# One quarter of the first block's first GEMM by seven products instead of eight

## The chip, the cores and the metric

The kernel runs on one core of a Trainium2 chip. The time is the device time of one execution, in microseconds (us). It is taken as the median of several runs. One more execution is recorded by the hardware profiler, and all rows and times of day ("at 38.21") below come from that one. The engines are TensorE (PE, with its weight loads as PEld), VectorE (DVE), ScalarE (ACT), GpSimd (POOL) and SyncE (SP, whose queue issues all DMAs here). Each engine works through its own list of instructions in order. An instruction that needs another engine's result waits for a semaphore.

## The reference

Two stages follow each other. First a retention (a linear attention with decay) over 4 batches, 8 heads, 768 positions and 64 dimensions:

```
state = gamma * state + k_t^T v_t
y_t   = scale * q_t state
```

Then y is laid out as x, with 3072 tokens of 512 values, and goes through two GEMMs with an ELU between them:

```
h = x @ w_in                      # 512 -> 2048
g = where(h > 0, h, exp(min(h, 0)) - 1)
out = g @ w_out                   # 2048 -> 512
```

All inputs are fp32, but for the weights, which the host hands over as raw float64 bits, two 32-bit words each.

## The kernel before

**Blocks and quarters.** The tokens are worked on in six blocks of 512. Each block has its retention, its first GEMM and its second GEMM. The hidden width of 2048 is cut for the first GEMM into four quarters, n = 0 to 3. A quarter pairs 256 hidden rows of the upper half (weights `w_a[n]`, row 0) with 256 of the lower half (`w_b[n]`, row 1), and each has the two halves of the 512 inputs. So a quarter is a two by two block product: hidden rows by inputs, with the block's tokens cut in two halves of 256 as the other factor.

**Seven products.** From the second block on, a quarter is computed by Strassen's scheme in Winograd's form: seven products M1 to M7 of 128x128 weights with 256 tokens, four matmuls each, where the plain way takes eight. It needs four sums of weights (s1 to s4, function `combine_w_in`, with s1 written over a21 in `w_b`, and s2, s3, s4 in `w_s`), four sums of x (t1 to t4, `combine_x_parts`), and sums of the products. Products accumulate in PSUM: M6 is added onto M1, M5 onto that, M3 onto that, all in one bank; M4 is added onto M7 in another. Between these steps ACT copies the bank's value out (`kept`), since other sums need it.

**The first block.** Here the kernel starts with nothing in place: weights arrive as 1 MB pieces of raw bits, and x comes out of the retention piece by piece. So the first GEMM of the first block is plain (`plain_first`). Its sixteen tiles, four a quarter, have 128 hidden values and 512 tokens each. Tiles 0 to 4 are begun with the first 256 tokens, as soon as the retention has made these, and finished with the others; tiles 5 to 15 are done at once. Their PSUM banks come from a pool with the tags a (two banks), b and d; tile 4 has one of four banks of the pool `ps_r`, which the retention's scores (sc), states (kv) and outputs (y) use in turn.

**ELU.** Each tile goes through `elu`: ACT takes relu(-h) and its exponential (lines 477 and 478, tile r), and DVE combines them with h (line 481). That last part is put one tile later in DVE's list than ACT's part, and only after it is the bank free.

**Weights.** Piece p (0 to 7 are `w_a[0]`, `w_b[0]`, `w_a[1]`, `w_b[1]` and so on; 8 to 15 belong to the second GEMM and are put into the first two parts of `w_s`) is loaded into one of three staging tiles. ACT prepares it with two operations (lines 164 and 166) and a third multiplication (line 168), which DVE does in its place where `by_vector` is set (line 190). DVE then decodes it (lines 191 and 194), and with that the staging tile is free for the load of the piece three further on.

**The order of the work** is written out by hand: the loop over the generator `inner` (`plain_first`) names for each tile n what else is put into the engines' lists after it: loads of the second block's q, k and v (`load`), the pieces (`next_piece`, which decodes one and prepares the next), the scaling of v on POOL (`scale_v`, line 281), the sums for the second GEMM (`inputs_of_first`), and the second block's scores, states and outputs at tiles 10 to 15. Then follows the first block's second GEMM (`second_of_first`, line 611), and after it the second block's first GEMM, whose quarters take their weight sums from `sides`. Before all this, PE does one matmul of 512 columns and 28 small ones on a tile of zeros, whose results nobody reads (lines 1106 and 1110).

Of the kernel before, what the change touches and what calls it, by code (L numbers as in the profile page):

```python
# [9 lines left out]
FP32 = mybir.dt.float32  # L10
# [4 lines left out]
ALU = mybir.AluOpType  # L15
# [3 lines left out]
def kernel(  # L19
# [32 lines left out]
    nc = tc.nc  # L52
    PSUM = bass.MemoryType.PSUM
    P = nc.NUM_PARTITIONS
# [5 lines left out]
    TH = TB // 2  # L60
# [14 lines left out]
    mpool = ctx.enter_context(tc.tile_pool(name="mpool", bufs=4))  # L75
# [3 lines left out]
    ps_r = ctx.enter_context(tc.tile_pool(name="ps_r", bufs=4, space=PSUM))  # L79
# [6 lines left out]
    so_ = t4.tile([P, 2, 7, 256], FP32, name="so")  # L86
# [35 lines left out]
    w_a, w_b, w_s = ([x[:, n] for n in range(NQ)] for x in (w_a_, w_b_, w_s_))  # L122
# [96 lines left out]
    begin = so_.rearrange("p n s c -> p (n s c)")  # L219
# [3 lines left out]
    for h in range(H):  # L223
# [11 lines left out]
        out=causal, in_=causal, compare_op=ALU.is_gt, fill=1.0, base=0, pattern=[[-1, P]], channel_multiplier=1  # L235
    )
    cmask = const.tile([P, D], FP32, name="cmask")
    for sub in range(2):
        r = slice(sub * D, (sub + 1) * D)
# [25 lines left out]
    xb = const.tile([P, 4, TB], FP32, name="xb")  # L265
    xt_ = const.tile([P, 4, 2, TH], FP32, name="xt")
    xt = [xt_[:, n] for n in range(4)]
# [3 lines left out]
    xt1 = [xb[:, n].rearrange("p (a t) -> p a t", a=2) for n in (1, 2, 3, 0)]  # L271
# [178 lines left out]

    half = [slice(0, TH), slice(TH, TB)]

    def combine_x_parts(tb=None):
        sub = lambda o, x, y: nc.vector.tensor_tensor(out=o, in0=x, in1=y, op=ALU.subtract)
        b11, b12, b21, b22 = (x_of(tb)[:, 2 * r : 2 * r + 2, half[t]] for r in range(2) for t in range(2))
        t1, t2, t3, t4_ = xt1 if tb == 1 else xt
        sub(t1, b12, b11)
        yield
        sub(t2, b22, t1)
        yield  # L460
        sub(t3, b22, b12)
        yield
        sub(t4_, b21, t2)
# [8 lines left out]
    def elu(g, h, depth=1, then=None):  # L472


        r = epool.tile([P, 512], FP32, name="r", tag="r", bufs=3)
        e = r if len(h.shape) == 2 else r.rearrange("p (a c) -> p a c", c=P)
        nc.scalar.activation(e, h, AF.Relu, scale=-1.0)  # L477
        nc.scalar.activation(e, e, AF.Exp, scale=-1.0)  # L478

        def last():  # L480
            nc.vector.scalar_tensor_tensor(g, e, -1.0, h, ALU.add, ALU.max)  # L481
            if then:
                then()

        while len(later) >= depth:
            later.pop(0)()
        later.append(last)

    def plain_first():

        tiles = [(n, w, row, fi) for n in range(NQ) for w, row in ((w_a, 0), (w_b, 1)) for fi in range(2)]
        banks = []

        def part(k, columns):
            n, w, row, fi = tiles[k]
            for j in range(4):
                nc.tensor.matmul(
                    banks[k][:, columns], lhsT=w[n][:, fi, j // 2, j % 2, :], rhs=xb[:, j, columns],
                    start=(j == 0), stop=(j == 3), skip_group_check=True,
                )  # L500

        for k in range(5):
            hp = bank("aabd"[k]) if k < 4 else ps_r.tile([P, 2, TH], FP32, name="hp", tag="r")
            banks.append(hp.rearrange("p a b -> p (a b)"))
            if k == 0:
                part(0, slice(0, C))
                yield
                part(0, slice(C, 2 * C))
            else:
                part(k, half[0])  # L510
            if k:
                yield
        for k in range(5):
            part(k, half[1])
            n, w, row, fi = tiles[k]
            elu(g_plain[row * NF + 2 * n + fi], banks[k])
            yield
        for k, (n, w, row, fi) in enumerate(tiles[5:]):
            hp = bank("aabd"[k % 4]).rearrange("p a b -> p (a b)")
            for j in range(4):  # L520
                nc.tensor.matmul(
                    hp, lhsT=w[n][:, fi, j // 2, j % 2, :], rhs=xb[:, j, :], start=(j == 0), stop=(j == 3)
                )
            elu(g_plain[row * NF + 2 * n + fi], hp)
            yield
        flush()

    def of_first(r, f, t, count=2):

        i = (r * NF + f) % 4  # L530
        g = gq[gnames[(r * NF + f) // 4]]
        return g[:, 2 * i + t] if count == 1 else g[:, 2 * i + t : 2 * i + 4 : 2, :]
# [112 lines left out]
    def combine_w_out(at, low, high):  # L645

        tt = lambda o, x, y, op: nc.vector.tensor_tensor(out=o, in0=x, in1=y, op=op)
        if at < 3:

            ms = [mpool.tile([P, 2, TH], FP32, name="m", tag="m") for _ in range(4)]  # L650
            ms = [m.rearrange("p a (b c) -> p (a b) c", c=P)[:, 0:3] for m in ms]
            ss = gq["T3"].rearrange("p (k f) (b c) -> p k (f b) c", k=4, c=P)
        else:
            ms, ss = (stage.tile([P, 4, 4, P], FP32, name="wi", tag="stage") for _ in range(2))
            ms = [ms[:, k, 0:3] for k in range(4)]
        ss = [ss[:, k] for k in range(4)]
        for first, dst, k in [(0, ms, 0), (3, ss, 1)][:: 1 if at < 3 else -1]:
            a11, a21, a12, a22 = (x[k][:, :, P * d : P * d + P] for x in (low, high) for d in range(2))
            s1, s2, s3, s4 = dst
            tt(s1, a21, a22, ALU.add)  # L660
            yield
            tt(s2, s1, a11, ALU.subtract)
            yield
            tt(s3, a11, a21, ALU.subtract)
            yield
            tt(s4, a12, s2, ALU.subtract)
            to = scratch2[first : first + dst[0].shape[1]].rearrange("j p (k f c) -> k f p j c", k=4, f=4)
            for k in range(4):
                to_send.append((to[k, at], dst[k]))
            yield  # L670

    def combine_w_in(n):

        tt = lambda o, x, y, op: nc.vector.tensor_tensor(out=o, in0=x, in1=y, op=op)
        a11, a12, a21, a22 = w_a[n][:, :, 0], w_a[n][:, :, 1], w_b[n][:, :, 0], w_b[n][:, :, 1]
        s2, s3, s4 = (w_s[n][:, j] for j in range(3))
        tt(s3, a11, a21, ALU.subtract)
        yield
        tt(a21, a21, a22, ALU.add)
        yield  # L680
        tt(s2, a21, a11, ALU.subtract)
        yield
        tt(s4, a12, s2, ALU.subtract)

    def bank(x):
        return ps_f.tile([P, 2, TH], FP32, name="p" + x, tag=x, bufs=2 if x == "a" else 1)

    def kept(ps):
        m = mpool.tile([P, 2, TH], FP32, name="m", tag="m")
        nc.scalar.copy(m, ps)  # L690
        return m
# [85 lines left out]
    for tb in range(1, NTB):  # L777
# [5 lines left out]
        for j in ORDER2:  # L783
            last = (4, 3) if j == 4 and tb == NTB - 1 else (3, 4)
# [321 lines left out]
            nc.tensor.matmul(warm[:, 0:n], lhsT=blank[:, 0:P], rhs=blank[:, 0:n], start=True, stop=True, skip_group_check=True)  # L1106

    unread(1, TB)
    for n in range(28):
        nc.tensor.matmul(  # L1110
            (warm, other)[n % 2][rows(n // 2 % 2), 0:D], lhsT=blank[rows(n % 2), 0:D], rhs=blank[rows(n % 2), 0:D],
            start=True, stop=True, skip_group_check=True,
        )
# [48 lines left out]
    y = outputs(0, 1)  # L1162
# [9 lines left out]
    def run(steps):  # L1172
        for _ in steps:
            pass

    def next_piece(by_vector=False):
        decode_all()
        prepare(by_vector=by_vector)
# [4 lines left out]
    def some(steps, count):  # L1183
        for _ in itertools.islice(steps, count):
            pass

    for n, _ in enumerate(inner):
        if n in (0, 2, 4):
            load(CPB + n // 2)
        if n == 4:  # L1190
            load(CPB + 3)
        if n in (1, 2, 4, 5, 7, 9):
            next_piece(n in (1, 2, 5, 7))
        if n in (3, 5, 7, 9):
            scale_v(CPB + (n - 3) // 2)
        if n == 4:
            run(inputs_of_first(0, [hslot() for _ in range(3)]))
        elif n == 10:
            scores(1, 0)
            scores(1, 1)  # L1200
        elif n == 11:
            states(1, 0)
            states(1, 1)
            next_piece()
            parts = sums_of_pieces(0)
            next(parts)
        elif n == 12:
            outputs_step(1, 0)
            run(parts)
            next_piece()  # L1210
        elif n == 13:
            outputs_step(1, 1)
            smalls = small_of_pieces(0)
            some(smalls, 3)
        elif n == 14:
            outputs_step(1, 2)
            some(smalls, 2)
            decode_all()
        elif n == 15:
            run(smalls)  # L1220
# [43 lines left out]
    def retention_step(tb, step):  # L1264
# [12 lines left out]
    tail = iter(())  # L1277
    last = held["last"]
    sides = [
        itertools.chain(combine_w_in(1), last), itertools.chain(combine_w_in(2), combine_w_in(3)), iter(()), iter(()),  # L1280
    ]
    smalls = {2: combine_small(2), 3: combine_small(3)}
    some(smalls[2], 1)
# [204 lines left out]
```

## Time and profile before

| what | us |
|---|---|
| median of three runs (lowest, highest) | 634.45 (632.83, 636.55) |
| the profiled execution | 632.87 |
| its span, first to last instruction | 630.9 |
| PE busy in the span | 624.8 |
| DVE, ACT, POOL busy | 483.1, 253.3, 21.8 |
| first block's first GEMM from tile 0's second half | 29.58 to 85.20 |
| first block's second GEMM begins | 85.20 |
| second block's first GEMM begins | 133.54 |

The span is what the profile covers; about 2 us lie outside it. A row of a timeline gives the start in us, the duration in us, the engine, the source line, the operation, what it writes and reads with its shape, and how many instructions are merged in the row. A bracket at its end gives the idle time before it and what ended that. An fp32 matmul appears as two records (x8 is four matmuls). A row's duration for PE includes the time for the last result to come out, so what counts is the distance from one start to the next. The tile names are those of the program, such as pa, pb and pd for banks with the tags a, b and d, hp for the bank of tile 4, and gC for the results of the ELU.

### The profile page before, as it was taken

How to read it: one execution, taken by the hardware profiler on the slowest of the kernel's cores; microseconds unless marked ns; L12 is line 12 of the kernel's file. 1: busy time of each engine (PE TensorE's matmuls, PEld its weight loads, DVE VectorE, ACT ScalarE, POOL GpSimd, SP SyncE). 2: the span in 40 equal slices, each digit the busy share in tenths (PEclk: the TensorE clock that was granted, in tenths of full speed). 3: DMA queues.
4: the chain of work that ended last, by engine and by line, in shares of the span. 5: the costliest groups of instructions: out<-in, count | busy, mean ns of one | idle time of the engine just before them, and what ended most of it. 6: DMA issues, size and time to landing. Idle time of an engine off the chain costs nothing.

```text
span 630.9 us, 16128 instructions
## 1 busy us (share of the span) xinstructions
PE 624.8 (99%) x6680; PEld 560.1 (89%) x6680; DVE 483.1 (77%) x884; ACT 253.3 (40%) x472; POOL 21.8 (3%) x25
## 2 busy tenths in 40 slices
PE   8999999999999999999999999999999999999998
PEld 5864578888899999889999989999988999988997
DVE  5779789989789675699685588777489877558975
ACT  6698635015541114653112646111465211366311
POOL 1021000000000000200000200000110000000000
PEclk9999999999999999999999999999999999999999
DMA  8698669689287888405888702888810798600794
GB/s 331 278 406 291 188 210 268 196 267 316 81 311 248 239 255 299 180 2 174 274 266 292 282 2 64 264 284 296 310 73 12 216 308 252 217 18 2 232 309 162
DMA packets 75897, 136.85 MB, mean 217 GB/s; under 512 B 6320, under 2 KB 31792, under 8 KB 70704
## 3 DMA queue, kind: packets, MB, share of 16 engines
q1 hardware_dynamic: 75824, 135.82, 64.8%
q8 instruction: 53, 0.87, 0.5%
q14 instruction: 20, 0.16, 0.1%
HBM read 114.56 MB, written 21.23 MB: 215 GB/s over the span
## 4 chain that ended last, share of the span: by engine, by line
PE 77%; SPq 1%; DVE 1%; DMA 1%; issue 0%; ACT 0%; ACTq 0%; DVEq 0%
PE pa L955 20%; PE pa L913 10%; PE pd L955 10%; PE pb L955 5%; PE pa L867 5%; PE pb L913 4%; PE pa L740 4%; PE qa L913 3%; PE pd L867 2%; PE qd L913 2%; PE pd L913 2%; PE pd L740 2%; PE y L394 1%; PE sc L307 1%; PE y L409 1%; PE kv L338 1%
## 5 line engine op out<-in xcount | busy, mean ns | idle before, releaser
L963 ACT COPY ms<-pa 128x128 f32<-128x128 f32 x104 | 27.7, 266 | 146.7 <-PE pa L955 146.7
L955 PE MATMUL pa<-ts,wq 128*128 128x128 f32 x560 | 74.2, 275 | 0.0
L955 PE MATMUL pd<-ts,wq 128*128 128x128 f32 x552 | 73.5, 276 | 0.0
L955 PEld LDWEIGHTS pa<-ts,wq 128*128 128x128 f32 x560 | 68.5, 192 | 0.4
L955 PEld LDWEIGHTS pd<-ts,wq 128*128 128x128 f32 x552 | 67.1, 192 | 0.6 <-DVE res L967 0.2
L955 PE MATMUL pa<-gC,wq 128*128 128x128 f32 x480 | 64.7, 278 | 0.0
L478 ACT ACTIVATE r<-r 128x512 f32<-128x512 f32 x96 | 60.5, 630 | 3.1
L955 PEld LDWEIGHTS pa<-gC,wq 128*128 128x128 f32 x480 | 59.0, 192 | 1.5 <-issue 0.3
L477 ACT ACTIVATE r<-gC 128x512 f32<-128x512 f32 x64 | 39.9, 624 | 32.4 <-DVE gC L921 32.4
L967 DVE TENSOR_TENSOR res<-pd,ms 128x128 f32<-128x128 f32 x68 | 19.5, 287 | 39.6 <-PE pd L955 38.4
L481 DVE SCALAR_TENSOR_TENSOR gC<-r,gC 128x512 f32<-128x512 f32 x64 | 44.0, 719 | 0.7 <-ACT r L478 0.7
L829 DVE TENSOR_TENSOR ts<-gC,ts 128x512 f32<-128x512 f32 x60 | 41.3, 688 | 1.0
L829 DVE TENSOR_TENSOR ts<-gC 128x512 f32<-128x512 f32 x60 | 41.0, 684 | 0.0
L281 POOL TENSOR_TENSOR chunk<-chunk,vf 128x512 f32<-128x512 f32 x16 | 20.0, 1251 | 428.8 <-DMA chunk<-in_qkv_dram 345.8
L955 PE MATMUL pb<-gC,wq 128*128 128x128 f32 x240 | 31.7, 275 | 0.0
L988 ACT COPY res<-pa 128x128 f32<-128x128 f32 x34 | 9.0, 266 | 55.0 <-PE pa L955 55.0
L955 PEld LDWEIGHTS pb<-gC,wq 128*128 128x128 f32 x240 | 29.2, 192 | 0.0
L690 ACT COPY m<-pa 128x512 f32<-128x512 f32 x24 | 13.9, 581 | 30.2 <-PE pa L740 16.3
L921 DVE TENSOR_TENSOR gC<-qa,gC 128x512 f32<-128x512 f32 x8 | 5.5, 692 | 25.0 <-PE qa L913 18.3
L913 PE MATMUL pa<-xt,w_b 128*128 128x256 f32 x96 | 23.0, 382 | 0.0
L913 PE MATMUL pa<-xt,w_s 128*128 128x256 f32 x96 | 23.0, 382 | 0.0
L913 PE MATMUL pa<-xb,w_a 128*128 128x256 f32 x96 | 22.7, 379 | 0.0
(255 smaller groups left out, 1244.3 us busy)
## 6 DMA issues: line engine op xcount, KB each, us to landing
wq<-scratch_dram SPq DMA_DIRECT2D x277, 256.0 KB, 4.3
chunk<-in_qkv_dram SPq DMA_DIRECT2D x23, 1024.0 KB, 8.6
wraw<-in_w_dram SPq DMA_DIRECT2D x15, 1024.0 KB, 6.0
out_dram<-res SPq DMA_DIRECT2D x14, 256.0 KB, 3.8
scratch_dram<-gT SPq DMA_DIRECT2D x12, 256.0 KB, 4.3
scratch_dram<-m SPq DMA_DIRECT2D x12, 192.0 KB, 6.0
scratch_dram<-so SPq DMA_DIRECT2D x4, 512.0 KB, 4.6
scratch_dram<-wi SPq DMA_DIRECT2D x2, 1024.0 KB, 6.4
```

Source lines behind the costliest of these rows:

```text
L281: eng.tensor_tensor(out=kv[:, 1], in0=kv[:, 1], in1=vf[:, i].unsqueeze(2).to_broadcast([C, H, D]), op=ALU.mult)
L477: nc.scalar.activation(e, h, AF.Relu, scale=-1.0)
L478: nc.scalar.activation(e, e, AF.Exp, scale=-1.0)
L481: nc.vector.scalar_tensor_tensor(g, e, -1.0, h, ALU.add, ALU.max)
L690: nc.scalar.copy(m, ps)
L740: nc.tensor.matmul(ps[:, fi, :], lhsT=w[:, fi, j2, :], rhs=x[:, j2, :], start=(begin and fi == 0 and j2 == 0), stop=(j2 == 1), skip_group_ ...
L829: sub = lambda o, x, y: nc.vector.tensor_tensor(out=o, in0=x, in1=y, op=ALU.subtract)
L867: nc.tensor.matmul(ps[:, f, :], lhsT=lhs[f], rhs=xs[j][k], start=(begin and f == 0), stop=True, skip_group_check=True,)
L913: nc.tensor.matmul(ps[:, fi, :], lhsT=w[:, fi, j2, :], rhs=x[:, j2, :], start=(j in (1, 7) and fi == 0 and j2 == 0), stop=(j2 == 1), skip_ ...
L955: nc.tensor.matmul(ps, lhsT=w[:, f, :], rhs=ts[j][k][:, f, :], start=(begin and f == 0), stop=(f == 3), skip_group_check=True,)
L963: nc.scalar.copy(m, ps)
L967: nc.vector.tensor_tensor(out=o, in0=x, in1=y, op=ALU.add)
```

## The change

The second quarter (tiles 4 to 7) of the first block is now computed by the seven products. A new function `quad_first` holds them. The banks of M1 and M2 come from `ps_r`, the bank of M7 and M4 has the tag a. The first halves (128 hidden values of each row pair) of M1 and M2 stand where tile 4's first half stood, before the second 256 tokens of x are there; the rest follows tiles 0 to 3. The sums of x are made into the tile `so`, which the sums of the second GEMM use later. The sums of weights are made by `combine_w_in(1)` during tiles 2 to 4. Since pieces of the second GEMM are later put over s2 and s3 in `w_s[1]`, these two are made again (`combine_w_in_again`) where `combine_w_in(1)` stood for the second block. Pieces are prepared and decoded at other tiles, and two instead of four of them have their multiplication on DVE. Ten of the 28 small matmuls at the start are gone.

```diff
-        for k in range(5):
-            hp = bank("aabd"[k]) if k < 4 else ps_r.tile([P, 2, TH], FP32, name="hp", tag="r")
-            banks.append(hp.rearrange("p a b -> p (a b)"))
+        for k in range(4):
+            banks.append(bank("aabd"[k]).rearrange("p a b -> p (a b)"))
...
-        for k in range(5):
+        quad = quad_first(1)
+        next(quad)
+        yield
+        for k in range(4):
             part(k, half[1])
             n, w, row, fi = tiles[k]
             elu(g_plain[row * NF + 2 * n + fi], banks[k])
             yield
-        for k, (n, w, row, fi) in enumerate(tiles[5:]):
-            hp = bank("aabd"[k % 4]).rearrange("p a b -> p (a b)")
+        for _ in quad:
+            yield
+        for k, (n, w, row, fi) in enumerate(tiles[8:]):
+            hp = bank("daab"[k % 4]).rearrange("p a b -> p (a b)")
...
+    x_first = [so_.rearrange("p n s c -> p (n s) c")[:, 2 * k : 2 * k + 2] for k in range(4)]
+
+    def quad_first(n):
+
+        a11, a12, s1, a22 = w_a[n][:, :, 0], w_a[n][:, :, 1], w_b[n][:, :, 0], w_b[n][:, :, 1]
+        s2, s3, s4 = (w_s[n][:, j] for j in range(3))
+        b11, b12, b21, b22 = (xb[:, 2 * r : 2 * r + 2, half[t]] for r in range(2) for t in range(2))
+        t1, t2, t3, t4_ = x_first
+        pairs = {1: (a11, b11), 2: (a12, b21), 3: (s4, b22), 4: (a22, t4_), 5: (s1, t1), 6: (s2, t2), 7: (s3, t3)}
+
+        def product(j, ps, begin, tiles=range(2)):
+            w, x = pairs[j]
+            for fi in tiles:
+                for j2 in range(2):
+                    nc.tensor.matmul(
+                        ps[:, fi, :], lhsT=w[:, fi, j2, :], rhs=x[:, j2, :],
+                        start=(begin and fi == 0 and j2 == 0), stop=(j2 == 1), skip_group_check=True,
+                    )
+
+        def use(r, t, h):
+            elu(of_first(r, 2 * n, t), h)
+
+        def with_kept(ps, m):
+            h = mpool.tile([P, 2, TH], FP32, name="m", tag="m")
+            nc.vector.tensor_tensor(out=h, in0=ps, in1=m, op=ALU.add)
+            return h
+
+        pa, pb = (ps_r.tile([P, 2, TH], FP32, name="hp", tag="r") for _ in range(2))
+        product(1, pa, True, [0])
+        product(2, pb, True, [0])
+        yield
+        product(1, pa, False, [1])
+        m1 = kept(pa)
+        product(2, pb, False, [1])
+        use(0, 0, with_kept(pb, m1))
+        product(6, pa, False)
+        u2 = kept(pa)
+        yield
+        pd = bank("a")
+        product(7, pd, True)
+        product(5, pa, False)
+        u4 = kept(pa)
+        use(1, 1, with_kept(pd, u4))
+        yield
+        product(3, pa, False)
+        use(0, 1, pa)
+        yield
+        product(4, pd, False)
+        use(1, 0, with_kept(pd, u2))
+        yield
+
+    def combine_w_in_again(n):
+
+        tt = lambda o, x, y, op: nc.vector.tensor_tensor(out=o, in0=x, in1=y, op=op)
+        s2, s3 = (w_s[n][:, j] for j in range(2))
+        tt(s2, w_b[n][:, :, 0], w_a[n][:, :, 0], ALU.subtract)
+        yield
+        tt(s3, w_b[n][:, :, 1], s2, ALU.subtract)
...
-    for n in range(28):
+    for n in range(18):
...
-        if n in (1, 2, 4, 5, 7, 9):
-            next_piece(n in (1, 2, 5, 7))
+        if n in (0, 4, 5, 6, 7, 9):
+            next_piece(n in (0, 4))
         if n in (3, 5, 7, 9):
             scale_v(CPB + (n - 3) // 2)
-        if n == 4:
+        if n == 0:
+            xparts, wparts = combine_x_parts(0, x_first), combine_w_in(1)
+        elif n == 1:
+            some(xparts, 2)
+        elif n == 2:
+            some(wparts, 2)
+        elif n == 3:
+            some(wparts, 1)
+            some(xparts, 1)
+        elif n == 4:
+            run(wparts)
+            run(xparts)
+        elif n == 6:
             run(inputs_of_first(0, [hslot() for _ in range(3)]))
...
-        itertools.chain(combine_w_in(1), last), itertools.chain(combine_w_in(2), combine_w_in(3)), iter(()), iter(()),
+        itertools.chain(combine_w_in_again(1), last), itertools.chain(combine_w_in(2), combine_w_in(3)), iter(()), iter(()),
```

Two smaller edits go with it: `combine_x_parts` takes the place for its results as an argument, and `elu` reshapes its tile to the form of h, whatever that is.

In the prediction, M1 to M7 are the products; h1, h2 and h3 are the three sums made by `with_kept` (M2 + m1, M7 + u4 and M4 + u2); m1, u2 and u4 are ACT's copies; "ELU k" is the pair of ACT operations of tile k and DVE's end of it.

More of the change, by code (lines that the diff above doesn't have):

```diff
@@ L451, with combine_x_parts @@
     half = [slice(0, TH), slice(TH, TB)]
-    def combine_x_parts(tb=None):
+    def combine_x_parts(tb=None, at=None):
         sub = lambda o, x, y: nc.vector.tensor_tensor(out=o, in0=x, in1=y, op=ALU.subtract)
         b11, b12, b21, b22 = (x_of(tb)[:, 2 * r : 2 * r + 2, half[t]] for r in range(2) for t in range(2))
-        t1, t2, t3, t4_ = xt1 if tb == 1 else xt
+        t1, t2, t3, t4_ = at or (xt1 if tb == 1 else xt)
         sub(t1, b12, b11)
@@ L475, in elu @@
         r = epool.tile([P, 512], FP32, name="r", tag="r", bufs=3)
-        e = r if len(h.shape) == 2 else r.rearrange("p (a c) -> p a c", c=P)
+        e = r if len(h.shape) == 2 else r.rearrange("p (a c) -> p a c", c=h.shape[-1])
         nc.scalar.activation(e, h, AF.Relu, scale=-1.0)
@@ L510, in plain_first @@
                 part(k, half[0])
-            if k:
                 yield
-        for k in range(5):
+        quad = quad_first(1)
+        next(quad)
+        yield
+        for k in range(4):
             part(k, half[1])
```

## The prediction

> **What bounds the kernel now.** First the page: the busy line, then the table of busy time by stretches, to see whether the stage of the change has idle time to win.
>
> ```profile
> span 630.9 us, 16128 instructions
> ...
> PE 624.8 (99%) x6680; PEld 560.1 (89%) x6680; DVE 483.1 (77%) x884; ACT 253.3 (40%) x472; POOL 21.8 (3%) x25
> ```
> ```profile
> 28.00:60.00 32.00, 32.00 (x168) 18.97 (x171) 25.46 (x34) 28.99 (x35) 6.31 (x4) 1.00 0.84 329
> 60.00:86.00 26.00, 26.00 (x466) 14.90 (x457) 20.59 (x38) 14.93 (x20) 0.00 (x0) 1.00 0.59 183
> 86.00:141.00 55.00, 54.91 (x255) 48.02 (x254) 50.97 (x78) 17.81 (x18) 0.00 (x0) 1.00 0.83 243
> ```
> Columns are us, then busy PE, weight load, DVE, ACT, POOL. From 28 us on PE never waits, so its work is the time: a product saved is time saved, a stall is time lost, one for one. But in 28 to 60, where the change lies, ACT is busy 28.99 of 32 us and DVE 25.46, and PE runs unhindered only because four rotating PSUM banks decouple it from them. Next the timelines of that stretch (start, us, engine, line, operation). PE:
>
> ```profile
> 36.49 1.89 PE L497 MATMUL hp<-xb,w_a 128*128 128x256 f32 x8
> 38.21 3.60 PE L521 MATMUL pa<-xb,w_a 128*128 128x512 f32 x8
> ...
> 55.38 3.60 PE L521 MATMUL pa<-xb,w_b 128*128 128x512 f32 x8
> 58.91 2.10 PE L307 MATMUL sc<-chunk 64*64 64x64 f32 x128
> 60.93 3.70 PE L521 MATMUL pb<-xb,w_b 128*128 128x512 f32 x8
> 64.56 2.08 PE L338 MATMUL kv<-chunk 64*64 64x64 f32 x112
> ```
> From start to start, four matmuls of 256 columns take 1.72, a tile of 512 columns 3.43. ACT:
>
> ```profile
> 34.40 1.15 ACT L164 ACTIVATE w_a<-wraw 128x1024 uint32<-128x1024 uint32 x1
> 35.59 1.39 ACT L166 ACTIVATE w_a<-wraw 128x1024 fp8e4<-128x1024 f32 x1
> 36.84 0.56 ACT L477 ACTIVATE r<-pb 128x512 f32<-128x512 f32 x1
> 37.43 0.63 ACT L478 ACTIVATE r<-r 128x512 f32<-128x512 f32 x1
> 37.97 1.14 ACT L164 ACTIVATE w_b<-wraw 128x1024 uint32<-128x1024 uint32 x1
> ...
> 57.56 1.18 ACT L164 ACTIVATE w_s<-wraw 128x1024 uint32<-128x1024 uint32 x1
> 58.78 1.39 ACT L166 ACTIVATE w_s<-wraw 128x1024 fp8e4<-128x1024 f32 x1
> 60.03 1.14 ACT L168 ACTIVATE wraw<-wraw 128x1024 f32<-128x1024 f32 x1
> 61.07 0.58 ACT L477 ACTIVATE r<-pa 128x512 f32<-128x512 f32 x1
> ```
> An ELU pair costs ACT 1.13 (36.84 to 37.97), a piece prepared in two operations 2.44 (34.40 to 36.84), in three 3.51 (57.56 to 61.07). DVE:
>
> ```profile
> 43.71 1.94 DVE L194 CUSTOM_DVE_ANT_0 w_b<-wraw,w_b 128x2048 uint16<-128x2048 uint16 x1
> ...
> 60.34 2.48 DVE L318 TENSOR_TENSOR chunk<-sc,cmask 128x512 f32<-128x512 f32 x4
> 62.74 0.68 DVE L481 SCALAR_TENSOR_TENSOR gC<-r,pa 128x512 f32<-128x512 f32 x1
> 65.76 0.43 DVE L350 TENSOR_TENSOR chunk<-kv,carry 128x256 f32<-128x256 f32 x1 [2.34 <-PE kv L338]
> ```
> The masks (L318) end at 62.8, PE's states (L338), which reuse the scores' PSUM tiles, begin at 64.56: a margin of 1.7 us. The same timeline gives an ELU's end 0.60 from start to start, an add or subtract of 128x512 0.61, or 0.72 when the next needs it, a decode 1.89 (33.40 to 35.29) and 2.60 with the multiplication on DVE (52.25 to 54.85). Handovers: PE's results reach ACT 0.2 after the last matmul's slot ends (29.58 plus 1.73, then ACT at 31.51), ACT's and DVE's reach others after 0.04.
>
> [...] here L829 and L561 take 684 to 690. [...] every start above follows program order, so an instruction that waits holds all behind it. [...] L194 at 43.71 took 1.94 instead of 1.23 while POOL worked from 43.01 to 44.57[...].
>
> **The change, part by part.** Removed from PE: tile 4 in two halves and tiles 5 to 7, 3.45 + 3 x 3.43 = 13.74. Added: seven products of 1.73, 12.09. Half of M1 and M2 takes the place of tile 4's first half, at 27.78, with the same columns. Unhindered, tile 8 would begin at 36.49 + 1.73 (the other halves) + 5 x 1.73 = 46.87 instead of 48.51: a credit of 1.64.
>
> But where tiles had banks of their own, M6, M5 and M3 accumulate in M1's bank, and ACT must have copied it before each. So I lay out the three queues in their new order, each start being the later of engine free and inputs ready. Until 30.2 nothing differs.
>
> M6 needs M1's copy, s2 and t2. ACT: ELU 0 at 31.51, then piece 4's two operations now stand ahead of ELU 1: 32.66 to 35.09, ELUs 1, 2, 3 to 38.54, M1's copy (0.58, as L690) done 39.1. DVE: piece 3 to 32.1, ELU 0 at 32.80, t1 and t2 to 34.8, then a wait for ELU 1's exponential till 36.38, s3 36.98, s1 37.70, ELU 2 38.31, s2 38.91 to 39.60. M6 starts at 39.64 and not 38.21: stall 1.43.
>
> M7 41.36 and M5 43.09 find all ready (t3 done 40.2, u2's copy 42.6). M3 waits for u4's copy: M5 ends 44.82, copied 45.02 to 45.60, M3 at 45.64: stall 0.82 (s4, behind piece 4's decode, is done 44.6). M4 47.36. Tile 8 49.09, tile 9 52.52, due to end at 55.95.
>
> Tile 10 needs the bank of M7 and M4, free only after the add h3 = M4 + u2. DVE: h2 45.64 (behind u4), an ELU, piece 5 to 49.46, an ELU to 50.06; piece 6 waits for ACT. ACT: ELU of h2 46.37, piece 6 47.52 to 51.1 with three operations. So piece 6 decodes 51.14 to 53.02, the four second-GEMM inputs to 55.79, h3 55.79 to 56.48, tile 10 at 56.52: stall 0.57. Scores 59.95, tile 11 61.97, its end 65.60.
>
> States need the masks done. ACT: ELU of M3 51.00, piece 7 52.15 to 55.63 (three operations, two before), ELU of h3 56.52, piece 8 57.67 to 61.15 (three, two before), ELU 8 61.15. DVE waits for that with tile 8's end till 62.44, then piece 8 63.04, ELU 9 64.92, masks 65.52 to 68.0. States begin at 66.84 (first two masks) and need the fourth 0.20 later: stall 1.24 + 0.20. Tile 12 starts at 69.04 where it was 66.57.
>
> Sum: 1.43 + 0.82 + 0.57 + 1.44 - 1.64 = +2.6 us. From here DVE has idle time (2.34 and more before L350, 1.99 before L384 at 81.34), the queues meet again at L384, and the second GEMM starts about 87.8 instead of 85.20. What follows is tied to it and shifts whole.
>
> Priced at nothing: (a) the weight loads on SP. Pieces 7 to 11 are asked for when 4 to 8 are decoded, at 43.96, 49.5, 53.1, 58.9, 65.0 (before 38.70, 45.71, about 51.1, 54.9, 59.8); at the page's 6.0 to landing they meet ACT's need at 52.15, 57.67, 63.45, 69.5, 74.1 with 2.2 us or more; behind a late one would queue an ELU and so tile 12. (b) the later weight combination, four DVE operations down to two: PE is busy 39.00 of 39.00 from 141 to 180, so the 2 x 0.69 show nowhere; without that cover they would give 1.4. (c) ten dummy matmuls: the first scores start at 5.15, when their chunk, issued at 0.74, landed (4.4 later). Dummies pass at about 0.03 a record, twenty records, so PE now idles from some 4.4 to 5.15. Below nothing isn't possible, as the chunk sets the start. [...] I take 0, since the hole is short. (d) POOL's blocking: four L281 of 1.3 to 1.8, seen to cost DVE 0.71 and 0.24; on the new path 0 to about 1.5; I take 0.
>
> **Rivals.** A, not slower: ACT and DVE keep up, no stall, -1.64, 632.8. For it, PE's earlier freedom; against, ACT's 90% in that stretch, with three copies of 0.58 and two L168 of 1.1 added. Each copy would have to be ready before its product, M1's 1.4 us earlier. B, slower: POOL's L281, whose chunks are now fetched ahead of piece 7, block DVE between 37.7 and 46, on the path to s2 and h2. At 0.71 a hit (L194 above) one or two hits add 0.7 to 1.4: +3.3 to +4.0, 637.8 to 638.5; it decides from 0.6 on. Against: in the trace two of four cost little. C, half the loss: DVE reaches the masks 1.4 us sooner, because piece 8 or ELU 8 goes faster than priced; then +1.2, 635.6. Against: three ACT operations at 3.5 are seen four times. That the saving isn't made can't be: four matmuls in 32 are gone.
>
> **How the numbers follow.** The profiled execution was 632.87 (span 630.9 and 2.0 around); it would be 635.5, span 633.5. The median of the runs, 634.45, lies 1.6 above it, so I predict 634.45 + 2.6 = 637.0. My case 0.60 (own range 635.6 to 638.2), B 0.17, C 0.16, A 0.04, a rest of 0.03 faster. About 0.5%, 3.2 us, is what can be told from no change: slower is B and the 0.18 of my case above 637.6, together 0.35; same 0.62; faster 0.03. The range 634.6 to 639.4 takes in C, B and the unpriced 1.4, and leaves out A.
>
> **What would show it.** PE idle of about 1.4 ahead of M6 (released by DVE or ACT), 0.8 ahead of M3 (ACT copy), 0.6 at tile 10 (DVE), 1.2 at the states (DVE L318); tile 8 starting near 49.1; the second GEMM near 87.8 and no new stall after. I am wrong if these sum to under 1.6, if kv after 7 us is slower than 0.69, or if DVE runs dry of slack between 86 and 141, where it is busy 93%.

## The result, and the profile after

| | before | changed |
|---|---|---|
| median, us (lowest, highest) | 633.95 (632.51, 636.55) | 639.18 (637.76, 641.29) |
| ratio, 95% interval | 1 | 1.009 (1.0069 to 1.011) |
| the profiled execution, span | 632.87, 630.9 | 640.92, 639.0 |

The changed kernel is slower by 0.9%, where I had called "no measurable difference" the likeliest case. The page of the changed kernel, the same lines as before:

```profile
span 639.0 us, 16131 instructions
...
PE 625.8 (98%) x6676; PEld 563.8 (88%) x6676; DVE 488.5 (76%) x891; ACT 256.7 (40%) x477; POOL 21.2 (3%) x25
```
PE issued four records fewer and yet was busy 1.0 us longer, and it was idle in the span for 639.0 - 625.8 = 13.2 us instead of 6.1. Where, the table by stretches tells (columns as in the prediction: the stretch, its length, busy PE, weight load, DVE, ACT and POOL, then the clock granted to PE, the DMA share and GB/s):

```profile
28.00:60.00 32.00, 28.88 (x155) 21.40 (x146) 27.05 (x38) 23.96 (x30) 5.50 (x4) 0.95 0.71 278
60.00:86.00 26.00, 25.01 (x463) 14.07 (x463) 22.18 (x39) 22.02 (x27) 0.00 (x0) 1.00 0.64 200
86.00:141.00 55.00, 54.44 (x292) 45.32 (x290) 47.89 (x73) 17.34 (x17) 0.00 (x0) 1.00 0.77 228
...
42.00:44.00 2.00, 1.98 (x6) 1.68 (x7) 2.00 (x4) 0.86 (x2) 0.00 (x0) 0.68 1.01 426
44.00:46.00 2.00, 2.00 (x6) 1.59 (x5) 1.93 (x3) 1.26 (x3) 0.75 (x1) 0.50 1.03 434
46.00:48.00 2.00, 2.00 (x10) 1.74 (x10) 2.00 (x3) 1.97 (x2) 1.44 (x2) 0.97 1.01 422
```
PE lacks 3.1 us between 28 and 60 and 1.0 between 60 and 86. And something appears that neither the busy columns nor the waits of another engine hold: from about 42 to 46 us the clock falls to half. Now PE's own timeline:

```profile
24.94 0.68 PE L394 MATMUL y<-chunk 64*64 64x64 f32 x26
27.02 0.75 PE L394 MATMUL y<-chunk 64*64 64x64 f32 x35 [1.40 <-issue]
...
38.00 1.89 PE L689 MATMUL hp<-xb,w_a 128*128 128x256 f32 x8
42.02 3.09 PE L689 MATMUL hp<-so,w_s 128*128 128x256 f32 x8 [2.13 <-DVE w_s L736]
44.91 2.49 PE L689 MATMUL pa<-so,w_s 128*128 128x256 f32 x8
...
49.80 1.99 PE L689 MATMUL hp<-xb,w_s 128*128 128x256 f32 x8 [0.68 <-ACT m L752]
...
60.72 3.70 PE L524 MATMUL pa<-xb,w_b 128*128 128x512 f32 x8 [0.33 <-DVE m L699]
...
70.52 0.33 PE L338 MATMUL kv<-chunk 64*64 64x64 f32 x4 [0.45 <-DVE chunk L318]
71.03 2.34 PE L338 MATMUL kv<-chunk 64*64 64x64 f32 x108 [0.17 <-DVE chunk L318]
...
91.93 1.24 PE L614 MATMUL x<-gC,w_s 128*128 128x256 f32 x5
...
141.24 1.99 PE L802 MATMUL pa<-xt,w_a 128*128 128x256 f32 x8 [0.81 <-DVE m L598]
148.93 1.35 PE L802 MATMUL pa<-xb,w_b 128*128 128x256 f32 x5 [0.51 <-ACT m L752]
```
In this order: M6 (42.02), M7 (44.91), M3 (49.80), tile 10 (60.72) and the states (70.52, 71.03) have the stalls that were forecast, with the forecast releasers. While M6 waited, PE started nothing else: from 40 to 42 us it has no matmul (busy 0.00, x0). M6 and M7 take 2.89 and 2.33 from start to start instead of 1.73: the half clock (0.68 from 42 to 44, 0.50 from 44 to 46). The row at 27.02 is new in kind. The bracket names no engine and no DMA: "issue" is time in which PE waited for nothing that the profile shows. It lies in the first block's outputs, where the change touched nothing; a smaller one, 0.44 us, stands at 13.41. The kernel before has in the same place:

```profile
24.81 1.50 PE L394 MATMUL y<-chunk 64*64 64x64 f32 x63
```
I cut each trace at two landmarks, the first matmul on the hp bank (the quarter's M1, before: tile 4) and the start of the second GEMM (91.93, before 85.20):

| stretch | before | changed | difference |
|---|---|---|---|
| start to the hp bank | 27.78 | 29.29 | +1.5 |
| hp bank to second GEMM | 57.42 | 62.64 | +5.2 |
| second GEMM to end | 545.70 | 547.07 | +1.4 |

Only the middle was in my sum, with +2.6. It holds the half clock as well, 1.76 us of it (2.89 + 2.33 - 2 x 1.73). The +1.4 at the end are nearly all in the two waits at 141.24 and 148.93 (0.81 + 0.51).

### The profile page after: what moved, and what is told of

It is laid out like the page before. It is cut to its first block, busy times and chain, and to the rows that moved or that the text cites. A ratio compares the mean times of both kernels' runs of the same rounds, so it can differ in the third digit from the quotient of the medians.

```text
span 639.0 us, 16131 instructions
## 1 busy us (share of the span) xinstructions
PE 625.8 (98%) x6676; PEld 563.8 (88%) x6676; DVE 488.5 (76%) x891; ACT 256.7 (40%) x477; POOL 21.2 (3%) x25
## 4 chain that ended last, share of the span: by engine, by line
PE 76%; SPq 1%; DVE 1%; DMA 1%; issue 0%; ACT 0%; ACTq 0%; DVEq 0%
PE pa L1017 20%; PE pa L975 10%; PE pd L1017 10%; PE pb L1017 5%; PE pa L929 5%; PE pb L975 4%; PE pa L802 4%; PE qa L975 3%; PE pd L929 2%; PE qd L975 2%; PE pd L975 2%; PE pd L802 2%; PE y L394 1%; PE sc L307 1%; PE y L409 1%; PE kv L338 1%
```

## The experiments

All ratios are to the kernel before, run on the same chip at the same time. Each profiled execution is cut at the same two landmarks (us):

| kernel | median | ratio (95%) | to hp | hp to 2nd GEMM | to end |
|---|---|---|---|---|---|
| changed, again | 640.90 | 1.0115 (1.010 to 1.013) | 29.30 | 61.14 | 548.1 |
| changed, 28 dummies | 639.35 | 1.0095 (1.006 to 1.013) | 27.29 | 61.26 | 549.9 |
| changed, first scaling on DVE | 640.66 | 1.0106 (1.008 to 1.013) | 29.52 | 60.59 | 548.1 |
| before, 18 dummies | 641.75 | 1.0147 (1.010 to 1.019) | 29.75 | 59.35 | 549.2 |
| changed, 28 dummies, 56 unread | 637.24 | 1.0055 (1.004 to 1.007) | 27.88 | 62.21 | 545.8 |
| before, 36 dummies | 635.58 | 1.0033 (1.002 to 1.005) | 29.10 | 57.49 | 547.3 |
| before, 92 dummies | 640.17 | 1.0099 (1.008 to 1.012) | 33.86 | 57.42 | 545.8 |
| changed, two wide fills | 638.48 | 1.0074 (1.005 to 1.010) | 29.08 | 61.14 | 546.2 |
| 56 unread, piece on DVE | 637.97 | 1.0048 (1.003 to 1.007) | 27.34 | 62.07 | 547.1 |
| and other banks | 638.29 | 1.0057 (1.004 to 1.008) | 27.62 | 62.16 | 546.5 |
| and a short fill | 637.07 | 1.0055 (1.004 to 1.007) | 27.30 | 61.00 | 546.0 |
| short fill, piece on DVE, banks as changed | 636.81 | 1.0046 (1.003 to 1.006) | 27.48 | 61.04 | 545.7 |

### The changed kernel again

No edit.

> The changed kernel once more, to see which parts of its loss repeat. If the parts are fixed by the program, PE again stands still 1.4 us within the outputs at L394 near 25.6 with nothing shown that it waits for, s2 (L736, the third) again takes about 1.5 where 0.69 is its price, M6 again starts about 2.3 late, and the second GEMM begins near 91.9. If they were the luck of that execution, these come out at 0, 0.69, 1.4 and near 88. The granted clock below 1 between 42 and 48 should appear only where M6 waits more than about 2 us.

M6's stall was 1.34 here, nearer the forecast 1.43, with s2 in 0.68 us and the clock at 1.0 throughout. In PE's timeline the unnamed gap came back in the same row (1.70 us), and another stood at 306.94:

```profile
27.02 0.75 PE L394 MATMUL y<-chunk 64*64 64x64 f32 x35 [1.70 <-issue]
...
306.94 0.33 PE L409 MATMUL y<-chunk 64*64 64x64 f32 x4 [0.98 <-issue]
```
The second GEMM began at 90.44, between the two places that I had expected. So the half clock comes in some executions only: the mean granted clock was 0.997 in two of the first nine runs and in one of the four here, else 1.0. The gap at 27 us repeats. The others don't have to: the one at 13.41 is absent here, the one at 306.94 was absent there.

### All 28 dummies with the quarter

```diff
-    for n in range(18):
+    for n in range(28):
```


> The changed kernel with all 28 small matmuls at the start. Theory F (fetch): ten matmuls fewer put every later PE instruction ten matmuls nearer to the start of the list, so that a fetch of PE instructions, a packet of 0.02 MB seen at 22 to 23 us before and at 24 to 25 after, is asked for later and PE runs dry; then here the gap of 1.4 us near 25.6 is gone, the tile before M6 starts at 27.8 instead of 29.3, and the time falls by about 1.4 us, a ratio near 1.006. Rival (the gap is a chance of DMA traffic, or the dummies keep the clock up): the gap stays, ratio 1.009; or the early rows before 9 us change speed.

The gap at 27 us is gone, the quarter begins at 27.29, and the second GEMM at 88.55. That is +3.35, or +3.84 counted from the hp bank, for the forecast +2.6. The expected ratio of 1.006 was missed (1.0095), since an unnamed gap came elsewhere, the last row here of PE's timeline:

```profile
39.46 1.97 PE L689 MATMUL hp<-so,w_s 128*128 128x256 f32 x8 [1.56 <-DVE w_s L736]
...
57.33 2.84 PE L524 MATMUL pa<-xb,w_b 128*128 128x512 f32 x6 [1.19 <-DVE m L699]
...
225.71 1.23 PE L1017 MATMUL pa<-gC,wq 128*128 128x128 f32 x8 [2.35 <-issue]
```
Following that gap the clock fell too (same kernel, by stretches):

```profile
226.00:228.00 2.00, 2.00 (x14) 2.00 (x14) 0.00 (x0) 0.27 (x1) 0.00 (x0) 0.67 0.04 13
228.00:230.00 2.00, 2.00 (x12) 2.00 (x11) 0.29 (x1) 0.00 (x0) 0.00 (x0) 0.50 0.57 153
```
At 225 us nothing of the change is left but a shift: PE's program is eight matmuls longer from the quarter on.

### The first scaling of v on DVE

```diff
-        if n in (3, 5, 7, 9):
+        if n in (5, 7, 9):
             scale_v(CPB + (n - 3) // 2)
+        if n == 7:
+            scale_v(CPB, True)
```


> The changed kernel with the first of the second block's four scalings of v taken from POOL and done by DVE behind piece 7's decode, where DVE stood idle 2.9 us. Theory P [...]: s2 took 1.49 because POOL worked from 40.28 to 41.32; without that it takes 0.69, M6 starts 0.8 sooner (stall 1.5 instead of 2.3), the clock then more seldom falls, and the time is 0.8 us lower (up to 2.5 in a profile where the clock fell before), ratio about 1.0075. Rival: s2 is slow for another reason (its operands), stays at 1.5 and nothing is gained.

POOL now starts at 47.07, behind s2, which took 0.68. M6 still waited 1.33, and the ratio is that of the changed kernel, not the expected 1.0075. Rival B, POOL blocking DVE, is not the loss: in the first profile s2 took 1.49 while POOL worked from 40.28 to 41.32, 0.8 us more than here. In the second profile of the changed kernel POOL worked from 40.79, and the operation that took longer (1.53) was the sum of x behind s2, which M6 does not wait for.

### The kernel before with 18 dummies

```diff
-    for n in range(28):
+    for n in range(18):
```


> The kernel before with 18 small matmuls in place of 28, the rest untouched. Theory F: PE's gap of about 1.4 us near 25.6 appears here too and goes straight into the time, ratio about 1.002 (635.4 against 634). Rival, as predicted: nothing, ratio 1.000, PE idle from 4.4 to about 5.

This run showed that the gaps need no quarter. No product, only ten matmuls fewer whose results nobody reads, and the kernel is 1.5% slower, no less than with the whole change (1.010 to 1.019 against 1.010 to 1.013 on the same chip). I had expected 1.002, with one gap. PE's timeline:

```profile
27.47 0.75 PE L394 MATMUL y<-chunk 64*64 64x64 f32 x35 [1.68 <-issue]
...
80.54 0.39 PE L409 MATMUL y<-chunk 64*64 64x64 f32 x10 [1.08 <-issue]
...
327.34 0.27 PE L409 MATMUL y<-chunk 64*64 64x64 f32 x2 [1.74 <-issue]
```
With two smaller gaps, 0.49 at 13.60 and 0.26 at 207.58, they make 5.25 of the 7.4 us that the span grew; half of the rest is in three waits of 0.3 to 0.5 us for VectorE and ScalarE. All gaps are in runs of 64x64 matmuls or, above, of 128x128 ones. The first is cut at the same record, 35 before the row's end, as in the changed kernel.

Theory F, which stands in its first form in the expectations above, now read so: PE's program itself comes from memory, in blocks, and where the end of a block falls among small matmuls, PE uses up instructions faster than the next block comes. What speaks for it in the profile of the changed kernel is a line in the queue table of the page, of a queue called q8 that carries instructions (packets, MB, share of the DMA engines):

```profile
q8 instruction: 53, 0.87, 0.5%
```
0.87 MB in 53 packets is 16.4 KB a packet. PE has 13608 records in this trace (6676 matmuls, 6676 weight loads, 256 others), 257 a packet. From these I took a block as 256 records, an estimate that the count below tests. An fp32 matmul is four of these records (two of each kind), so such a block holds 64 matmuls. In the scores' row of the prediction (58.91) 64 small ones pass in 2.02 us, while 64 matmuls of 256 columns take 64 x 0.43 = 28 us. The packets move with the program. This is the DMA view of the kernel before from 22 to 23 us, then of the changed kernel from 24 to 25 us, the second before the gap:

```profile
q1 hardware_dynamic: 52, 0.40, 95.6%
q8 instruction: 1, 0.02, 6.7%
```
```profile
q1 hardware_dynamic: 49, 0.39, 94.0%
q8 instruction: 1, 0.02, 6.7%
```
One packet takes 6.7% of sixteen engines over 1 us, which is 1.07 us of one engine, while the loads of q1 take the other 94%.

That these packets are PE's blocks can be counted in the fourteen traces themselves. Number PE's records in each trace from 0 in the order of their starts. Each of the 18 gaps marked "issue" stands ahead of a record whose number leaves the remainder 193 when it is divided by 256, so all of them lie at ends of the same blocks. Now set the first q8 packet beside the block that begins at record 449 (193 + 256), the second beside the next, and so on. Of the 734 blocks of all traces, none begins earlier than 1.22 us after its packet has landed, and each of the 18 gaps ends 1.25 to 1.61 us after that landing. In the changed kernel the packet lasted from 24.66 to 25.73, PE was through with the block before it at 25.39, and the new block began at 27.01. In the kernel before the packet for the same block landed at 23.72, ahead of the old block's last record at 24.93. The next runs test the theory by moving the block ends.

### The shift made whole: 56 unread matmuls ahead of M6

```diff
-    for n in range(18):
+    for n in range(28):
...
+        pd = bank("a")
+        for i in range(56):
+            nc.tensor.matmul(
+                pd[rows(i % 2), 0, 0:D], lhsT=blank[rows(0), 0:D], rhs=blank[rows(0), 0:D],
+                start=True, stop=True, skip_group_check=True,
+            )
         product(6, pa, False)
         u2 = kept(pa)
         yield
-        pd = bank("a")
```


> The changed kernel with all 28 dummy matmuls at the start and 56 unread 64x64 matmuls ahead of product M6, inside the stall there. Theory F (PE's program comes in blocks of 16 KB, 64 of these matmuls each; a boundary that falls among small matmuls leaves PE dry): ahead of the quarter PE's program then stands as in the kernel before, behind it 8 + 56 = 64 matmuls later, one whole block, so every boundary again falls where it did. No gap over 0.3 us without a named releaser after 20 us, the second GEMM at 88 to 90, and only the queue's stalls and the fill are left: 636 to 637.5 us, ratio 1.004 to 1.007. Rival S (the quarter itself costs later, through banks, DMAs or the m tiles): as with 28 dummies alone, 639 to 640.

The page's busy line of this kernel:

```profile
PE 628.3 (99%) x6808; PEld 567.1 (89%) x6808; DVE 489.0 (77%) x891; ACT 256.8 (40%) x477; POOL 20.0 (3%) x25
```
6808 records are 64 matmuls more than before's 6680. In PE's timeline no unnamed gap over 0.3 us is left, and the stretch from the second GEMM on takes 545.8 as in the kernel before (545.7). With more work on PE than any of the kernels above, it has the lowest median of those with the quarter; its interval of the ratio (1.004 to 1.007) touches that of 28 dummies alone (1.006 to 1.013). Rival S, a later cost of the quarter through banks or DMAs, falls.

### The kernel before with 36 and with 92 dummies

```diff
-    for n in range(28):
+    for n in range(36):
```


> The kernel before with 36 dummy matmuls instead of 28: no product of the quarter, but everything from there on stands 8 matmuls later, as it does behind the quarter with 28 dummies. Theory F: an unnamed gap of 2 to 2.5 us near 219 to 224 us (products of gC and wq), possibly a further one ahead of it, and 636 to 638 us, ratio 1.004 to 1.008. Rival D (it is the number of dummies that keeps the clock up, and fewer are dear): eight more cost their own 0.2 us at most, 633.2 to 634.0.

PE's timeline of this kernel:

```profile
223.15 0.83 PE L955 MATMUL pa<-gC,wq 128*128 128x128 f32 x6 [1.38 <-issue]
```
The gap came where theory F had put it, in the kernel without any quarter, with 1.38 instead of 2 to 2.5 us, and a second of 0.85 at 24.28. The time, 635.58, is 0.4 below the expected lower end. Eight further dummies are not free, so rival D falls.

For the 92 dummies the same line has `range(92)`.

> The kernel before with 92 dummy matmuls: 64 more, one whole block in theory F. Every boundary falls where it did, so no unnamed gap over 0.3 us after 20 us; the start is later by at most the 64 matmuls' own 1.4 us: 633.4 to 635.3 us, ratio 1.000 to 1.003. Rival (28 was a tuned value and any other number costs several us, as 18 did): 638 or more.

The time missed the expectation by 5 us and lies in the range of the rival. The place of the loss did not contradict the theory. From the hp bank on this execution repeats the kernel before (57.42 and 545.8 us, no unnamed gap). All 6.1 us are lost ahead of it. The first scores began at 7.11 instead of 5.15, and the states were cut in PE's timeline:

```profile
11.20 0.63 PE L338 MATMUL kv<-chunk 64*64 64x64 f32 x27 [2.56 <-issue]
```
A whole block of small matmuls at the start is used up faster than the next comes: PE was through with it at 8.42, and the next block's packet landed at 9.69. Behind the gap the clock was at half from 12.4 to 19.2 us, seen in the table by stretches as a mean of 0.87:

```profile
14.00:34.00 20.00, 19.41 (x429) 14.72 (x430) 14.21 (x34) 10.54 (x14) 0.30 (x1) 0.87 0.68 250
```
I had priced the 64 matmuls at their own time; by theory F they use up PE's program as well. That 28 would be the only good number is not what the two runs say: eight more cost 1.7 us, 64 more 6.3, and in both traces the unnamed gaps stand at block ends.

### Two wide fills ahead of M6

```diff
+        pd = bank("a")
+        for _ in range(2):
+            nc.tensor.matmul(
+                pd.rearrange("p a b -> p (a b)"), lhsT=blank[:, 0:P], rhs=blank, start=True, stop=True, skip_group_check=True
+            )
         product(6, pa, False)
         u2 = kept(pa)
         yield
-        pd = bank("a")
```


> The changed kernel (18 dummies) with two unread matmuls of 512 columns ahead of product M6, in its stall, so PE isn't idle there. Theory F with the clock: the unnamed gap of 1.4 to 1.7 us near 26 stays (nothing ahead of it is moved), behind the quarter PE's program stands where it stood in the kernel before (10 fewer, 8 and 2 more), so no gap near 307; the clock stays above 0.9 from 42 to 46 us: 637 to 639 us, ratio 1.006 to 1.009. If neither the clock nor the place in the program matters: 639.5 to 641, as the changed kernel, or 0.2 more.

As theory F had it: the gap near 26.8 stays (1.39), there is none near 307, the clock is 1.0 from 40 to 46, and M6 and M7 take 1.73 and 1.80 from start to start. The ratio of 1.0074 (1.005 to 1.010) is below that of the changed kernel's repetition (1.0115), but its interval overlaps that of the first measurement (1.009). So the two traces show that a gap went and the clock stayed up; the gain in time, some 1 to 2.5 us, is less sure.

### The queue's own stalls

First the piece at n = 7, on the kernel with 28 dummies and 56 unread matmuls:

```diff
-            next_piece(n in (0, 4))
+            next_piece(n in (0, 4, 7))
```


> The changed kernel with 28 dummies and the 56 unread matmuls ahead of M6, and the preparation of w's piece at the pass n = 7 given to VectorE instead of ScalarE, as in the kernel before. If the idle 0.47 + 0.17 us at the states of 68.7 us is ScalarE's longer preparation, it goes: 0.6 to 1.0 us less than without this edit (637.24), 636.2 to 636.7 us, ratio 1.004. Rival (the masks are late because VectorE has more to do in all): unchanged or worse, 637.2 to 638.

PE's timeline of this kernel:

```profile
68.50 2.35 PE L338 MATMUL kv<-chunk 64*64 64x64 f32 x108 [0.17 <-DVE chunk L318]
...
305.01 0.34 PE L409 MATMUL y<-chunk 64*64 64x64 f32 x7 [0.81 <-issue]
```
Of the states' stall the larger part (0.47) is gone, as expected, but the medians, 637.24 and 637.97 on two chips, show no gain. The second row says why for the profiled execution: an unnamed gap came at 305, although PE's program stands as before there. So the place of the block ends is not all; when the block arrives counts as well. Here its packet landed at 303.47 and PE was through with the block before at 303.98; without this edit the packet had landed at 300.44, and PE was through at 304.31. The packet had started 5.26 us after PE entered the block before, against 1.82. Why it started so much later stays open.

Then M3 and tile 10 in other banks. Here the result that M3 completes (row 0, second 256 tokens) gets M3 alone, without the sum of M1, M6 and M5; this kernel and the next leave that sum out, so their output lacks it:

```diff
-        product(3, pa, False)
-        use(0, 1, pa)
+        pc = bank("b")
+        product(3, pc, True)
+        use(0, 1, pc)
...
-            hp = bank("daab"[k % 4]).rearrange("p a b -> p (a b)")
+            hp = bank("daba"[k % 4]).rearrange("p a b -> p (a b)")
```


> As the kernel with the piece on VectorE, and M3 writes a free bank (b) instead of waiting for the copy of M5 out of its own, and tile 10 takes bank b instead of the one that M4's sum still reads. If the stalls of 0.68 and 0.33 us are these banks and nothing else is late behind them, both go: 1.0 us less again, 635.2 to 635.8 us, ratio 1.002 to 1.003. Rival (ScalarE and VectorE are behind by themselves, the wait only moves to the next bank): 636.2 to 636.7 as without it, with the idle time at tile 9 to 12.

PE's timeline of this kernel:

```profile
59.55 0.67 PE L524 MATMUL pb<-xb,w_b 128*128 128x512 f32 x1 [1.97 <-DVE gC L481]
```
A miss: M3's wait went, and tile 10 waits 1.97 us for the end of M3's ELU in its new bank. The rival was right, the queues behind are late and the wait only moves; 638.29 is above even the rival's 636.2 to 636.7.

The same with the fill spread over two banks:

```diff
-        pd = bank("a")
+        pd, pc = bank("a"), bank("b")
...
-                pd[rows(i % 2), 0, 0:D], lhsT=blank[rows(0), 0:D], rhs=blank[rows(0), 0:D],
+                (pd, pc)[i % 2][rows(i // 2 % 2), 0, 0:D], lhsT=blank[rows(i % 2), 0:D], rhs=blank[rows(i % 2), 0:D],
...
-        pc = bank("b")
```


> As the kernel with other banks, the 56 unread matmuls spread over two banks and four quadrants, so that they take about 1.3 us instead of 3.4 and M6 starts near 39.8 instead of 41.8 us. All of the quarter's own terms are then out except the fill: 637.24 - 0.64 - 1.01 - 2.0 = 633.6 us, 633.2 to 634.3, ratio 0.999 to 1.001. Rival (something else of the change costs 1 us or more that no idle time of PE names): 634.6 or more.

M6 started at 40.32 instead of 41.81 and the second GEMM at 88.30 instead of 89.78, but 1.74 us of stall stayed at tile 10, so 637.07 is well above the expected 633.6. Last, the complete quarter with this fill, the piece on DVE, and M3 and tile 10 in the banks of the change:

> The changed kernel, complete, with 28 dummies, the 56 unread matmuls spread over two banks ahead of M6, and the one piece prepared on VectorE; M3 and tile 10 are again where the change puts them. Against the kernel with the long fill (second GEMM at 89.41) M6 starts 1.5 to 2 us earlier and nothing else is moved: stalls of 0.7 at M3, 0.3 to 1.2 at tile 10 and 0.2 at the states stay, the second GEMM begins at 87.3 to 88.3, and the time is 635.2 to 636.5 us, ratio 1.002 to 1.004. Rival (the quarter's three queues are not decoupled: what M6 gains is lost at tile 10): the second GEMM at 88.8 to 89.5 and 637 to 638. An unnamed gap of 0.3 to 0.9 us near 305, as with the long fill, would add itself to either.

PE's timeline of this kernel:

```profile
40.51 1.99 PE L689 MATMUL hp<-so,w_s 128*128 128x256 f32 x8
...
57.63 2.84 PE L524 MATMUL pa<-xb,w_b 128*128 128x512 f32 x6 [0.41 <-DVE m L699]
...
88.52 1.89 PE L614 MATMUL x<-gC,w_s 128*128 128x256 f32 x8
```
M6 gained 1.0 us, not 1.5 to 2, and the second GEMM 0.9; 636.81 is 0.3 above the expected range. There is no unnamed gap, the last stretch is 545.7 as before, and the ratio 1.0046 (1.003 to 1.006) is what the quarter costs with its fill and with this piece on VectorE. No version tried beats the kernel before.

## Why the prediction was wrong

- **The credit and the queues** (the part by part sum): right in place and releaser, too small in sum. With no gap ahead of it (28 dummies), tile 8 began at 49.11, forecast 49.09, but this agreement is luck in part: the hp bank began 0.49 earlier than in the kernel before, and counted from there tile 8 came after 21.82 for the forecast 21.31. The states' stall was 0.63 of idle time for the forecast 1.44, but M6's and tile 10's were larger. From the hp bank to the second GEMM the quarter cost +3.8 for the forecast +2.6. The term that was too small is tile 10: 57.33 - 52.54 is 4.79 from tile 9's start, 1.36 over a tile's 3.43, for 0.57 forecast; in the first profile it is 0.50, so it varies from one execution to the next. M6 came 12.17 after the hp bank, for 11.86 forecast. The sum has a small slip as well: its own rows put tile 12 2.47 late (69.04 - 66.57), not 2.6, because 3.43 stands for tile 10 where the step to the scores was 3.53 before.
- **"(c) ten dummy matmuls", value 0, bound 0 to 1.4: the step that failed.** The 1.4 was my own estimate of a lower clock, and it was not shown: from 6 to 10 us the granted clock was 1.00 in the changed kernel as before, and kv after 7 us indeed stayed at 0.69. The 0 rested on the sentence "below nothing isn't possible, as the chunk sets the start". But their removal moves PE's whole program against the blocks of theory F. Alone it costs 8.4 us (641.75 - 633.37), with gaps at 27, 80 and 327 us, two of them outside the stretches that I examined. None of the three signs of being wrong that I had named came.
- **"What follows is tied to it and shifts whole": failed, mostly for the same reason.** With ten dummies out and eight matmuls in, everything behind the quarter stands two matmuls earlier; with 28 dummies, eight later. Both brought gaps (at 307 in two of three profiles, and at 225 with 2.35 us and a clock drop). The first profile has no such gap there; it lost its 1.4 in the waits at 141 and 149. With the shift made up to 64, the last stretch takes the 545.8 us that it should. So of the changed kernel's loss, about 3 us are the quarter (637.24 and 636.81 against 633.8 to 633.9, fill included), and the rest, 2 to 4 us, is the place of PE's program with the waits and half clocks that come behind the gaps. The two parts do not add: quarter alone +6.0, dummies alone +8.4, both +7.5 on one chip.
- **(d) POOL, and rival B:** rightly taken at 0 for the median. In the first profile it did hit s2 (1.49 for 0.68), lengthened the idle time ahead of M6 to 2.13 us, and the half clock behind it cost 1.76 more. The half clock is not in every execution: the granted clock was 0.997 in two of nine runs and 1.0 in the others.
- **(a) and (b)**, weight loads and the later weight combination: no run speaks against zero. In the first profile PE waited 0.81 and 0.51 at 141 and 149 for DVE and ACT, but the kernel before with 18 dummies has the same two waits, 0.29 at 137.90 and 0.51 at 145.59, without the quarter, and with 28 dummies the changed kernel has neither. What brings them is not shown.
- **Rivals A and C** fell, as stalls of all four kinds came; of C it is true that the masks came earlier than priced, but tile 10 lost more. None of my rivals was the cause, and that the range of 634.6 to 639.4 held the time was luck: its upper end was drawn for B. What would have led there: I read the brackets of rows that wait for an engine, and saw PE never idle after 28 us. The row of 63 outputs at 24.81 took 1.50, where the changed kernel with 28 dummies took 1.30 for the same row; that, and a queue called "instruction" on the page, stood in the profile before.

## What to carry to other kernels

A change of the number of instructions on an engine can itself be a change, as taking out ten unread matmuls was here, at 8.4 us: where runs of very short instructions leave little time per instruction (here 64 matmuls in 2.02 us), count how far everything behind is shifted, look for "issue" gaps there, and compare against a kernel that has the same shift and nothing else. Before judging the change itself, make one more control: add unread work, in a wait, that brings the count back to a whole block (here 56 matmuls, 64 with the quarter's eight, after which the last stretch took 545.8 us for 545.7). In these runs the product saved did not pay, as its handovers (copies of an accumulating bank) left PE without work: the seven products saved 1.64 us of work and, with 28 dummies, lost 3.84 + 1.64 = 5.5 us in waits that the plain tiles did not have (4.06 us of it in the brackets of PE's rows).

## What the runs showed of the hardware

- Ten unread matmuls fewer, 0.03 us a record, cost 8.4 us; eight more cost 1.7 (635.58 - 633.89), 64 more 6.3. Adding 56 unread ones to the kernel with 28 dummies took the ratio from 1.0095 to 1.0055, about 2.5 us, with intervals that just touch.
- The queue q8 carried 0.87 MB in 53 packets in the changed kernel, 16.4 KB a packet and one for every 257 of PE's 13608 records. Of 734 blocks of 256 records in fourteen traces none began sooner than 1.22 us after its packet had landed. 64 small matmuls, a block, passed in 2.02 us in the kernel before.
- Unnamed gaps measured 0.26 to 2.56 us, all at block ends, within or at the edge of runs of 64x64 or 128x128 matmuls, never among those of 256 or 512 columns. In two profiles of the changed kernel one gap stood in the same place (27.02, with 1.40 and 1.70 us), while one of 0.44 at 13.41 and one of 0.98 at 306.94 stood in one of them each.
- After idle times of 2.13 (changed), 2.35 (28 dummies) and 2.56 us (92 dummies) the clock granted to PE went to 0.50, for 3.41, 3.41 and 6.83 us; after those of 1.3 to 1.97 us it stayed at 1.0. With unread matmuls in the wait the clock stayed at 1.0 in all six profiles; as it also did in two without them, where the wait was 1.33 and 1.34 us, the runs do not show that the fill is what kept it.
